# Spins into any idle bank, a first layer opened block by block, and later sums of weights, in a fused attention and feed-forward kernel

## The chip, the cores and the metric

The kernel runs on one core of one Trainium2 chip. The metric is the device time of one execution in microseconds. A core has five engines with queues of their own, which run in order and meet at semaphores: TensorE (PE in the profile; PEld is its loading of weights), VectorE (DVE), ScalarE (ACT), GpSimd (POOL) and SyncE (SP, which here issues the transfers). TensorE writes to eight banks of PSUM, b0 to b7, each of 512 columns of fp32; VectorE and ScalarE read them.

## The reference

```python
def _attn_ref(q, k, v, omega):          # batch 8, heads 8, 576 positions, head_dim 64, 128 features
    scale = 1.0 / np.sqrt(np.sqrt(D))
    q_s, k_s = (q * scale, k * scale)
    def phi(x):
        proj = np.einsum('bhsd,md->bhsm', x, omega)
        sq = np.sum(x * x, axis=-1, keepdims=True) / 2.0
        h = proj - sq
        h = h - np.max(h, axis=-1, keepdims=True)
        return np.exp(h) / np.sqrt(m)
    q_p, k_p = (phi(q_s), phi(k_s))
    kv = np.einsum('bhsm,bhsd->bhmd', k_p, v)
    z = np.sum(k_p, axis=2)
    num = np.einsum('bhsm,bhmd->bhsd', q_p, kv)
    den = np.einsum('bhsm,bhm->bhs', q_p, z)[..., None] + 1e-06
    return (num / den)
...
    xn = (x - mu) / np.sqrt(var + 1e-06) * g_ln      # x: 4608 rows of 512, the heads side by side
    ch = np.maximum(xn @ w_ch1, 0.0) @ w_ch2         # 512 -> 2048 -> 512
    return (x + ch)
```

## The kernel before, in words

The 4608 rows of x are worked in nine tiles of 512, each in four chunks of 128. For a tile, attention makes its part of x (keys: projection, maximum, exponent, products with the values into `kv`; queries: projection, a copy out of PSUM, a maximum over all partitions by GpSimd's all-reduce, a subtraction, an exponent, then the products with `kv` and a division). Then x is centred, turned (by TensorE in the first tile, line 1397) and split into a high and a low part, and the two layers follow. A matrix product in fp32 is made of three products of such parts. The weights come packed and are unpacked by VectorE and ScalarE, block by block: a block of w1 is 128 rows, `w1_00` to `w1_30` are the four that the first matmuls need. From the third tile on a scheme with seven products in place of eight is used (`seven`, line 1510), and for it sums of the w1 weights are made once (`gen_sides`, lines 496, 507 and 529) and kept in memory.

The order of every engine's work is made when the program is built, by a small scheduler (`Plan`). Each piece of work is a Python generator that yields what it needs: a result (`wait`), a buffer (`get`), or an engine with an estimated cost (`run`). Among what can start first on an engine, the lowest rank goes first. `plan.places` holds the free buffers, with the time since when each is free; `plan.cur.end` is the scheduled end of the work at hand. On the chip the engines then run that order and wait at semaphores, so the scheduler's costs set the order, not the time.

Until the first layer starts (`mlp_on`), TensorE's idle time is filled with spins: matmuls of a constant tile (`spin`, line 370) whose output nobody reads. `gen_warm` issues them one by one while nothing else could start, with a cost of 0.29 in the first 5 us and 0.11 later, and a single one follows most groups of products. They write `pw`, a tile in the last bank, which no other work may use until then.

The first layer of the first tile begins in `opening` (line 1448): four blocks of 128 hidden columns (`f`), each in its own bank, for the first two chunks of x (`j` = 0) and then for the last two. It waits for all four blocks of w1 before its first matmul. Later blocks of the first layer come from `mm1` (by `rounded`, line 1421, with 512 columns at once, or split into two matmuls of 256 columns at line 1480).

Of the kernel before, what the change touches and what calls it, by code (L numbers as in the profile page):

```python
# [12 lines left out]
F32 = mybir.dt.float32  # L13
# [6 lines left out]
PE, ACT, DVE, POOL, SP = "PE", "ACT", "DVE", "POOL", "SP"  # L20
PSUM = bass.MemoryType.PSUM

P = 128
# [5 lines left out]
NK = DM // P  # L29
# [6 lines left out]
T = 512  # L36
# [3 lines left out]
QB = 256  # L40
# [28 lines left out]
class Plan:  # L69
# [78 lines left out]
    def free(self, *names):  # L148
        for n in names:
            assert n not in self.places, n  # L150
            self.places[n] = self.cur.seen()
            self.cur.holds -= n[0] == "b" and 0 < self.cur.holds
            self.wake(lambda w: w[0] == "get" and n in w[1])
# [59 lines left out]
def favor_ffn(ctx, tc, kT, kTr, kD, kDr, vF, vR, qT, qD, omT, gT, w1, w2, out):  # L213
# [12 lines left out]
    nc = tc.nc  # L226
# [4 lines left out]
    ps = ctx.enter_context(tc.tile_pool(name="ps", bufs=1, space=PSUM))  # L231
    dp = ctx.enter_context(tc.tile_pool(name="dp", bufs=1, space=bass.MemoryType.DRAM))
    plan = Plan()
    free, done = plan.free, plan.done
# [16 lines left out]
    def us(eng, t):  # L251
        return "run", {eng: t}
# [16 lines left out]
    def wait(*key):  # L269
        return "wait", key  # L270

    def names(tag, n):
        return plan.own(*(f"{tag}{i}" for i in range(n)))

    def tile_of(tag, shape, dtype=F32, pool=None):
        pool = pool or (wp if tag[1].isdigit() and tag[0] == "w" else small if tag[0:2] in ("kv", "mb", "st") or tag[0] == "v" else sb)
        return pool.tile(shape, dtype, tag=tag, name=tag, bufs=1)
# [20 lines left out]
    banks = names("b", 8)  # L298
    plan.own("one", "two")
    b_at, b_h, b_acc = banks[0:2], banks[2:4], banks[4:8]  # L300
    mlp_on = []
# [27 lines left out]
    spin = const.tile([P, 2 * P], BF16, name="spin")  # L329
# [32 lines left out]
    nc.scalar.dma_start(g_sb, gT)  # L362
    nc.scalar.preload_act_table_set("natural_log_exp_and_others")

    pw = tile_of(banks[-1], [P, 512], F32, ps)[:, 0 : 2 * P]

    def warm(n):
        if not mlp_on:
            for _ in range(n):
                nc.tensor.matmul(pw, spin[:, 0:P], spin, start=True, stop=True)  # L370

    def gen_const():
        yield dma(P * M)
# [24 lines left out]
    wparts = {}  # L398
# [85 lines left out]
    def gen_sides(g, k):  # L484


        yield wait("xnT", SEVEN - 1, TC - 1)
        if g + k:
            yield wait("read", *((g, 0) if k else (g - 1, 1)))
        tags, parts = [], []  # L490
        for row in (k, k + 2):
            tags.append((yield "get", n_big))
            parts.append(tile_of(tags[-1], [P, 2, HC], F32R))
            yield dve2(DM)
            w = wparts[1, NK * g + row]
            nc.vector.tensor_tensor(out=f32(parts[-1]), in0=f32(w[:, :, 0]), in1=f32(w[:, :, 1]), op=ALU.add)
        for _ in range(2):
            tags.append((yield "get", n_big))
            parts.append(tile_of(tags[-1], [P, 2, HC], F32R))
        low, high, a, b = parts  # L500
        low, high, a, b = f32(low), f32(high), f32(a), f32(b)
        for out, left, right, op in (
            (a[:, 0], low[:, 1], high[:, 1], ALU.add), (a[:, 1], low[:, 0], low[:, 1], ALU.subtract),
            (b[:, 0], a[:, 0], low[:, 0], ALU.subtract), (b[:, 1], high[:, 0], b[:, 0], ALU.subtract),
        ):
            yield dve2(HC)
            nc.vector.tensor_tensor(out=out, in0=left, in1=right, op=op)
        if (g, 0) not in sides:
            sides[g, 0] = dp.tile([P, 4, 2, 2, 2, P], F32, tag=f"side{g}", name=f"side{g}", bufs=1)
        done(("read", g, k))  # L510
        for n in range(2):
            plan.add(plan.cur.rank, halved(g, k, n, tags[n], tags[2 + n], (a, b)[n]))
# [198 lines left out]
    def gen_k(b, c, kraw, v, early, t_v, n_kp):  # L711
# [52 lines left out]
        def side(s, t_b, pk):  # L764
# [3 lines left out]
            )  # L768
            if (b, c) in WIDE:
                o = kp[:, 4 * s : 4 * s + 4]  # L770
# [241 lines left out]
    def features(blk, j, s, t_b, pq):  # L1012
        t_c = yield "get", n_big
        qc = tile_of(t_c, [P, 2 * QB])
        eng = yield "run", {ACT: 0.48, DVE: 0.62} if blk >= T // QB else {ACT: 0.58}
        copy(eng, qc, pq)
        direct = blk < T // QB
        if not direct:
            free(t_b)
        mx_turn = yield "get", turn["mx"]  # L1020
        t_m = yield "get", n_big
        mx = tile_of(t_m, [P, 2 * QB])
        yield us(POOL, 1.8)
        nc.gpsimd.partition_all_reduce(mx, qc, P, bass_isa.ReduceOp.max)  # L1024
        done(("mx", blk, j, s))
        yield dve(2 * QB) if direct else dve2(2 * QB)
        nc.vector.tensor_tensor(out=qc, in0=pq if direct else qc, in1=mx, op=ALU.subtract)  # L1027
        if direct:
            free(t_b)
        free(t_m, mx_turn)  # L1030
        yield act(2 * QB, 1, 0.13)
        nc.scalar.activation(out=qc, in_=qc, func=AF.Exp)  # L1032
        phis[blk, j, s] = t_c, qc.rearrange("p (a b) -> p a b", b=QB)
        done(("phi", blk, j, s))
# [374 lines left out]
    def passes(x):  # L1409
        return x.rearrange("p (a c b) -> p c a b", b=BW, c=4)  # L1410
# [15 lines left out]
    def opening(count):  # L1426


        for k in range(NK):
            yield wait("w", 1, k)  # L1430
        ph = []
        for j in range(2):
            for i in range(2):
                yield wait("xnT", 0, 2 * j + i)
            if not mlp_on:
                mlp_on.append(True)
            xnT = xnTs[0][1]
            for f in range(count):
                if j == 0:
                    t_b = yield "get", b_h if f >= count - len(b_h) else b_acc  # L1440
                    ph.append((t_b, bank(t_b)))
                out = passes(ph[f][1])[:, :, 8 * j : 8 * j + 8]
                cs = slice(f % 2 * P, (f % 2 + 1) * P)
                for k in range(NK):
                    yield us(PE, 3 * 0.1134)
                    w = wparts[1, k][:, f // 2]
                    for l, r in ((0, 0), (1, 0), (0, 1)):
                        nc.tensor.matmul(  # L1448
                            out, w[:, l, cs],
                            passes(xnT[:, r, k])[:, :, 8 * j : 8 * j + 8],  # L1450
                            start=j + k + l + r == 0, stop=j == 1 and k == NK - 1 and r == 1, skip_group_check=True,
                        )
                if j == 1:
                    done(("mm1", 0, f))
                    plan.add(MOST_URGENT, relu(0, f, *ph[f]))
        in_order[0] = IN_ORDER
        paired(LONG)

    def mm1(t, f):
        for k in range(NK):  # L1460
            yield wait("w", 1, f // NK * NK + k)
        for i in range(TC):
            yield wait("xnT", t, i)
        if not mlp_on:
            mlp_on.append(True)
        t_x, xnT = xnTs[t]
        t_b = yield "get", b_h
        ph = bank(t_b)
        for k in range(NK):
            yield us(PE, 3 * 0.225)  # L1470
            w = wparts[1, f // NK * NK + k][:, f % NK // 2]
            cs = slice(f % 2 * P, (f % 2 + 1) * P)
            for l, r in ((0, 0), (1, 0), (0, 1)):
                first, last = k + l + r == 0, k == NK - 1 and r == 1
                if (t, f) < NARROWED and (fast[0] or locked[0] < 1) or as_rows(2 * ENOUGH):
                    rounded(ph, w[:, l, cs], xnT[:, r, k], start=first, stop=last, mixed=t == NARROWED[0], lies="a c b")
                    continue
                paired(2)
                for n in range(2):
                    nc.tensor.matmul(  # L1480
                        passes(ph)[:, :, 8 * n : 8 * n + 8], w[:, l, cs],
                        passes(xnT[:, r, k])[:, :, 8 * n : 8 * n + 8],
                        start=first and n == 0, stop=last, skip_group_check=True,
                    )
        if f == NF - 1:
            free(t_x)
        done(("mm1", t, f))
        plan.add(MOST_URGENT, relu(t, f, t_b, ph))
# [425 lines left out]
            free(t_x)  # L1914

    def gen_warm():
        plan.places.pop(banks[-1])
        plan.cur.after = 1.0
        while not mlp_on:
            cold = plan.cur.end < COLD  # L1920
            yield us(PE, 0.29 if cold else 0.11)
            warm(1)
            plan.cur.after = plan.cur.end + (0.0 if cold else WARM)
        free(banks[-1])

    def gen_mlp():
        last = []
# [54 lines left out]
        plan.add(min(rank, FRONT.get((n, f), rank)), gen_w(n, f, rank))  # L1982
    for g in range(NK):
        for k in range(2):
            plan.add(RSIDE + g, gen_sides(g, k))
        plan.add(URGENT, gen_move(g))
    for f in SHARED:
        plan.add(URGENT, gen_return(f))
# [40 lines left out]
LEAVE, RSIDE = 24, 24  # L2029
# [29 lines left out]
RX = -1100  # L2059
AHEAD = 0  # L2060
XACT = 3
WIDE = ((0, 0), (0, 2))
HELD = {0: (None, ("mx", 0, 0, 0)), 1: (("mx", 0, 1, 0), ("mx", 0, 1, 1)), 2: (None, None), 3: (None, None)}
RFIRST, BEHIND = (-35, -27.5), -33

# [50 lines left out]
```

## Time and profile before

| | |
|---|---|
| median of 3 runs | 909.66 us (909.53 to 909.95) |
| the profiled execution | 909.5 us, span 907.7 us |
| TensorE busy | 902.0 us (99%) |
| VectorE busy | 777.1 us (86%) |
| ScalarE busy | 543.2 us (60%) |
| GpSimd busy | 138.2 us (15%) |

The span is the time from the first to the last instruction of the profiled execution. Matmuls are pipelined and their ends are modelled in the profile, so a busy TensorE is one that has a matmul under way, not one at its peak. The granted clock of TensorE is 1.0 of full speed over the whole span.

### The profile page before, as it was taken

To read this page: it belongs to the slowest core of one execution; us is meant where nothing else is said; L and a number is where in the kernel's file an instruction comes from. 1 tells how busy PE (TensorE), PEld (TensorE's weight loads), DVE (VectorE), ACT (ScalarE), POOL (GpSimd) and SP (SyncE) were. 2 spreads that over 40 slices of the span, in tenths; PEclk is the share of its full clock that TensorE was granted. 3 is DMA by queue.
4 is the path that set the end of the run, shared out by engine and by line. 5 is a ranking of instruction groups with operands and counts; after the bars stand their busy time and mean duration, and the time that the engine had idled before them with its cause. 6 is when DMAs were issued, how large, how long until landed. Compare 5 with 4: busy or idle time off the path is not lost.

```text
span 907.7 us, 21830 instructions
## 1 busy us (share of the span) xinstructions
PE 902.0 (99%) x8159; PEld 822.2 (91%) x8159; DVE 777.1 (86%) x1799; ACT 543.2 (60%) x1303; POOL 138.2 (15%) x107
## 2 busy tenths in 40 slices
PE   9999999999999999999999999999999999999998
PEld 7888788888899999998999999999999999999998
DVE  6999988989888899779898998888878788778767
ACT  7988876546566477546774666556555553453442
POOL 4201503300112042000220131002301400000000
PEclk9999999999999999999999999999999999999999
DMA  9199665558898898988999988889777869998981
GB/s 349 70 352 363 242 201 173 150 146 261 291 349 287 281 366 270 307 296 288 299 338 310 329 278 273 307 296 357 233 230 237 292 180 325 374 318 295 360 293 48
DMA packets 153146, 249.92 MB, mean 275 GB/s; under 512 B 13264, under 2 KB 66640, under 8 KB 153040
## 3 DMA queue, kind: packets, MB, share of 16 engines
q1 hardware_dynamic: 152752, 248.45, 81.2%
q8 instruction: 65, 1.06, 0.5%
q14 instruction: 41, 0.34, 0.1%
q10 hardware_dynamic: 288, 0.07, 0.0%
HBM read 205.47 MB, written 42.99 MB: 274 GB/s over the span
## 4 chain that ended last, share of the span: by engine, by line
PE 96%; DVE 2%; DMA 1%; ACT 0%; issue 0%; ACTq 0%; DVEq 0%
PE b L1421 38%; PE b L1510 29%; PE b L1794 7%; PE b L1759 6%; PE b L827 4%; PE b L1187 4%; PE b L865 2%; PE b L909 2%; PE b L1448 1%; PE b L370 1%; PE b L957 1%; PE b L1099 1%; DVE v L1847 0%; DVE kp L1903 0%; DMA hid<-omT 0%; DMA w<-side 0%
## 5 line engine op out<-in xcount | busy, mean ns | idle before, releaser
L1421 PE MATMUL b<-w,hid 128*128 128x512 f32 x1090 | 261.9, 385 | 0.0
L1421 PEld LDWEIGHTS b<-w,hid 128*128 128x128 f32 x1090 | 198.9, 188 | 34.0 <-issue 0.3
L1024 POOL PARTITION_ALL_REDUCE wide<-wide x72 | 134.8, 1893 | 473.8 <-ACT wide L259 271.4
L1510 PE MATMUL b<-xnT,w 128*128 128x256 f32 x1344 | 174.0, 276 | 0.0
L1510 PEld LDWEIGHTS b<-xnT,w 128*128 128x128 f32 x1344 | 164.3, 188 | 2.8
L1510 PE MATMUL b<-w,w 128*128 128x256 f32 x1008 | 126.1, 276 | 0.0
L1574 DVE TENSOR_TENSOR w<-b,w 128x256 f32<-128x256 f32 x224 | 108.7, 485 | 15.9 <-PE b L1510 10.4
L1510 PEld LDWEIGHTS b<-w,w 128*128 128x128 f32 x1008 | 120.5, 188 | 1.5 <-DVE w L1574 0.3
L880 ACT ACTIVATE kp<-kp,mb 128x128 f32<-128x128 f32 x184 | 66.9, 397 | 34.0 <-DVE mb L877 33.7
L1421 PE MATMUL b<-xnT,w 128*128 128x512 f32 x324 | 79.4, 387 | 0.0
L1421 PEld LDWEIGHTS b<-xnT,w 128*128 128x128 f32 x324 | 59.7, 187 | 12.0 <-issue 1.0
L1032 ACT ACTIVATE wide<-wide 128x512 f32<-128x512 f32 x72 | 45.4, 635 | 37.7 <-DVE wide L1027 37.7
L1759 PE MATMUL b<-w,hid 128*128 128x256 f32 x460 | 64.4, 279 | 0.0
L1759 PEld LDWEIGHTS b<-w,hid 128*128 128x128 f32 x460 | 57.6, 188 | 1.4
L1600 ACT ACTIVATE hid<-w 128x256 fp32r<-128x256 f32 x85 | 40.4, 513 | 30.4 <-DVE w L1574 24.7
L259 ACT COPY wide<-b 128x512 f32<-128x512 f32 x69 | 39.4, 586 | 28.5 <-PE b L1421 20.0
L1794 PE MATMUL b<-w,wide 128*128 128x256 f32 x408 | 52.4, 275 | 0.0
L1602 DVE SCALAR_TENSOR_TENSOR hid<-w,hid 128x256 fp32r<-128x256 f32 x85 | 48.3, 586 | 4.1 <-ACT hid L1600 3.3
L1027 DVE TENSOR_TENSOR wide<-wide,wide 128x512 f32<-128x512 f32 x64 | 47.0, 743 | 3.6 <-POOL wide L1024 3.4
L986 DVE TENSOR_TENSOR wide<-wide,wide 64x512 fp32r<-64x512 f32 x56 | 40.8, 734 | 9.7 <-ACT wide L984 8.2
L1794 PEld LDWEIGHTS b<-w,wide 128*128 128x128 f32 x408 | 49.1, 188 | 0.0
L886 ACT COPY kp<-b 128x256 f32<-128x256 f32 x92 | 31.4, 368 | 24.0 <-PE b L865 23.8
(171 smaller groups left out, 1453.6 us busy)
## 6 DMA issues: line engine op xcount, KB each, us to landing
w<-side SPq DMA_DIRECT2D x224, 256.0 KB, 5.0
w<-kept SPq DMA_DIRECT2D x80, 512.0 KB, 5.2
w<-kept SPq DMA_DIRECT2D x67, 256.0 KB, 5.2
w<-w SPq DMA_DIRECT2D x32, 512.0 KB, 7.2
wide<-qD SPq DMA_DIRECT2D x56, 256.0 KB, 5.3
w<-deep SPq DMA_DIRECT2D x47, 256.0 KB, 5.5
wide<-kD SPq DMA_DIRECT2D x40, 256.0 KB, 5.1
kept<-w SPq DMA_DIRECT2D x16, 512.0 KB, 3.9
```

The lines of the kernel that those rows point to most:

```text
L880: nc.scalar.activation(out=kp[:, j], in_=kp[:, j], func=AF.Exp, scale=1.0, bias=mb[:, j : j + 1])
L986: nc.vector.tensor_tensor(out=qs[D:P], in0=qraw[D:P], in1=f32(qs[D:P]), op=ALU.subtract)
L1024: nc.gpsimd.partition_all_reduce(mx, qc, P, bass_isa.ReduceOp.max)
L1027: nc.vector.tensor_tensor(out=qc, in0=pq if direct else qc, in1=mx, op=ALU.subtract)
L1032: nc.scalar.activation(out=qc, in_=qc, func=AF.Exp)
L1421: nc.tensor.matmul(out.rearrange(f"p ({lies}) -> {order}", a=AW, b=BW), lhsT, rhs.rearrange(f"p (a c b) -> {order}", a=AW, b=BW), start=st ...
L1510: nc.tensor.matmul(passes(out), left(k, l), passes(right[:, r, k]), start=start and k + l + r == 0, stop=k + r == 2, skip_group_check=True,)
L1574: nc.vector.tensor_tensor(out=out, in0=left, in1=right, op=ALU.add)
L1600: nc.scalar.activation(out=hl[:, 0, cols], in_=x, func=AF.Relu)
L1602: nc.vector.scalar_tensor_tensor(out=hl[:, 1, cols], in0=x, scalar=0.0, in1=f32(hl[:, 0, cols]), op0=ALU.max, op1=ALU.subtract)
L1759: nc.tensor.matmul(accs[i].rearrange("p (c a b) -> p c a b", a=AW, b=BW)[:, :, n * 8 : n * 8 + 8], hl[:, l, cs], w[:, r, n * HC : (n + 1) ...
L1794: nc.tensor.matmul(out.rearrange("p (c a b) -> p c a b", a=8, b=8), left[:, l, chunk * P : (chunk + 1) * P], right[:, r].rearrange("p (a c ...
```

## The change

Spins get a new tile in the bank that has been free longest, by the scheduler's times, and are left out where no bank is free; the last bank is no longer set aside. A query copy of the first tile may also go to VectorE. `opening` waits for each block of w1 before the matmuls of that block and goes block by block in its first half; `mm1` waits likewise. The ranks of the sums of w1 weights are 12 apart instead of 1. In the first batch, key chunk 3 instead of chunk 2 gets the exponent in one wide piece (`WIDE`).

```diff
-    pw = tile_of(banks[-1], [P, 512], F32, ps)[:, 0 : 2 * P]
-
-    def warm(n):
-        if not mlp_on:
+    def warm(n, at=0.0):
+        idle = [] if mlp_on else [x for x in banks if plan.places.get(x, 1e9) <= plan.cur.end - at]
+        if n and idle:
+            to = bank(min(idle, key=plan.places.get), 2 * P)
             for _ in range(n):
-                nc.tensor.matmul(pw, spin[:, 0:P], spin, start=True, stop=True)
+                nc.tensor.matmul(to, spin[:, 0:P], spin, start=True, stop=True)
...
-        eng = yield "run", {ACT: 0.48, DVE: 0.62} if blk >= T // QB else {ACT: 0.58}
+        eng = yield "run", {ACT: 0.48, DVE: 0.62} if blk >= T // QB else {ACT: 0.58, DVE: 0.62}
...
     def opening(count):
-        for k in range(NK):
-            yield wait("w", 1, k)
...
-            for f in range(count):
+            places = [(k, f) for k in range(NK) for f in range(count)]
+            for k, f in places if j == 0 else sorted(places, key=lambda x: x[1]):
                 if j == 0:
+                    yield wait("w", 1, k)
+                if j == k == 0:
...
     def mm1(t, f):
-        for k in range(NK):
-            yield wait("w", 1, f // NK * NK + k)
...
         for k in range(NK):
+            yield wait("w", 1, f // NK * NK + k)
...
     def gen_warm():
-        plan.places.pop(banks[-1])
...
-            yield us(PE, 0.29 if cold else 0.11)
-            warm(1)
+            cost = 0.29 if cold else 0.11
+            yield us(PE, cost)
+            warm(1, cost)
             plan.cur.after = plan.cur.end + (0.0 if cold else WARM)
-        free(banks[-1])
...
-            plan.add(RSIDE + g, gen_sides(g, k))
+            plan.add(RSIDE + 12 * g, gen_sides(g, k))
...
-WIDE = ((0, 0), (0, 2))
+WIDE = ((0, 0), (0, 3))
```

On TensorE, at the very start, the first spins of the kernel before (`b7_93` is the one tile that all of them write; `DVE_49` is VectorE's semaphore):

```order
L370 LDWEIGHTS spin_74 [waits DVE_49]
L370 MATMUL b7_93<-spin_74 128x256
L370 LDWEIGHTS spin_74
L370 MATMUL b7_93<-spin_74 128x256
L370 LDWEIGHTS spin_74
L370 MATMUL b7_93<-spin_74 128x256
```

The same place in the change (`b0_114`, `b0_116` and so on are new tiles in one bank, b0; `PE_49` is TensorE's own semaphore):

```order
L370 LDWEIGHTS spin_74 [waits DVE_49]
L370 MATMUL b0_114<-spin_74 128x256
L370 LDWEIGHTS spin_74
L370 MATMUL b0_116<-spin_74 128x256 [waits PE_49]
L370 LDWEIGHTS spin_74
L370 MATMUL b0_119<-spin_74 128x256 [waits PE_49]
L370 LDWEIGHTS spin_74
L370 MATMUL b0_121<-spin_74 128x256 [waits PE_49]
```

There are 13 spins at this place in both; eleven of them now wait for a value of TensorE's semaphore that the spin just before sets (the first has none before it, and at the tenth the bank changes).

On TensorE, ahead of the fifth product of x (line 1099), the end of a burst of 17 spins in the kernel before:

```order
L370 LDWEIGHTS spin_74
L370 MATMUL b7_93<-spin_74 128x256
L370 LDWEIGHTS spin_74
L370 MATMUL b7_93<-spin_74 128x256
L1099 MATMUL b0_594<-kv0_94,wide2_335 64x65 [waits Activation_49]
```

And in the change, the end of a burst of 18 at the same place:

```order
L370 LDWEIGHTS spin_74
L370 MATMUL b0_570<-spin_74 128x256 [waits PE_49]
L370 LDWEIGHTS spin_74
L370 MATMUL b3_575<-spin_74 128x256 [waits DVE_49]
L370 LDWEIGHTS spin_74
L370 MATMUL b3_577<-spin_74 128x256 [waits PE_49]
L370 LDWEIGHTS spin_74
L370 MATMUL b3_580<-spin_74 128x256 [waits PE_49]
...
L1099 MATMUL b0_594<-kv0_93,wide2_352 64x65 [waits Activation_49]
```

The bursts are about as long as before here, and 16 of the 18 spins wait for the one before. In the whole program there are 64 spins instead of 101: 13, 5, 18, 8 and 9 in bursts and 11 single ones.

On TensorE, where the first layer opens, before:

```order
L1397 MATMUL b5_712<-ident_76,wide10_693 128x128 x3
L1448 MATMUL b6_710<-xnT0_624,w1_00_369 128x4x8x8 [waits DVE_49,PE_49]
L1448 MATMUL b6_710<-xnT0_624,w1_00_369 128x4x8x8
L1448 MATMUL b6_710<-xnT0_624,w1_00_369 128x4x8x8 [waits DVE_49]
L1448 MATMUL b6_710<-xnT0_624,w1_10_493 128x4x8x8 x3
L1448 MATMUL b6_710<-xnT0_624,w1_20_539 128x4x8x8 x3
L1448 MATMUL b6_710<-xnT0_624,w1_30_625 128x4x8x8 x3
```

And in the change:

```order
L370 MATMUL b6_721<-spin_74 128x256 [waits PE_49]
L1448 MATMUL b6_724<-xnT0_627,w1_00_452 128x4x8x8 [waits PE_49,Activation_49]
L1448 MATMUL b6_724<-xnT0_627,w1_00_452 128x4x8x8
L1448 MATMUL b6_724<-xnT0_627,w1_00_452 128x4x8x8 [waits DVE_49]
L1448 MATMUL b4_734<-xnT0_627,w1_00_452 128x4x8x8 x3
L1448 MATMUL b2_739<-xnT0_627,w1_00_452 128x4x8x8 x3
L1448 MATMUL b3_743<-xnT0_627,w1_00_452 128x4x8x8 x3
L1448 MATMUL b6_724<-xnT0_627,w1_10_517 128x4x8x8 x3
```

One block of w1 now serves four banks before the next block is touched, a burst of 9 spins stands just ahead, and the transposes of the third chunk (line 1397), ahead of the opening before, come after its first 24 matmuls.

## Rows read from the trace of the kernel before

**Rows 1.** The page: busy time, share of the span; granted clock in 40 slices.
```profile
PE 902.0 (99%) x8159; PEld 822.2 (91%) x8159; DVE 777.1 (86%) x1799; ACT 543.2 (60%) x1303; POOL 138.2 (15%) x107
...
PEclk9999999999999999999999999999999999999999
```

**Rows 2.** All waits of TensorE: us in total, times, longest.
```profile
PE b L370 <- DVE spin L330: 1.2, 1, 1.2
PE b L1397 <- ACT wide L1262: 0.2, 1, 0.2
```

**Rows 3.** The chain of waits in order of time: start us, us, what.
```profile
42.07 8.52 PE b L1448 x75
...
210.37 25.11 PE b L1421 x114
...
558.79 2.73 PE b L1510 x24
```

**Rows 4.** Timeline of TensorE from the start: start us, us, instructions.
```profile
1.19 2.95 PE L370 MATMUL b<-spin 128*128 128x256 bf16 x13 [1.19 <-DVE spin L330]
4.22 1.85 PE L909 MATMUL b<-om,w 64*128 64x128 f32 x16
5.91 1.03 PE L957 MATMUL b<-wide,om 64*128 64x256 f32 x8
6.78 2.49 PE L909 MATMUL b<-om,w 64*128 64x128 f32 x32
```

**Rows 5.** Timeline of TensorE, 24 to 52 us.
```profile
25.53 1.48 PE L370 MATMUL b<-spin 128*128 128x256 bf16 x12
26.95 0.69 PE L1099 MATMUL b<-kv,wide 128*64 128x65 f32 x16
...
30.06 2.03 PE L370 MATMUL b<-spin 128*128 128x256 bf16 x17
32.02 0.69 PE L1099 MATMUL b<-kv,wide 128*64 128x65 f32 x16
...
34.30 0.28 PE L370 MATMUL b<-spin 128*128 128x256 bf16 x1
34.42 0.60 PE L1397 MATMUL b<-ident,wide 128*128 128x128 f32 x4
...
35.57 1.27 PE L370 MATMUL b<-spin 128*128 128x256 bf16 x10
36.67 0.60 PE L1397 MATMUL b<-ident,wide 128*128 128x128 f32 x4
37.11 1.25 PE L370 MATMUL b<-spin 128*128 128x256 bf16 x10
...
38.98 2.64 PE L1448 MATMUL b<-xnT,w 128*128 128x256 f32 x21
```

**Rows 6.** Timeline of all engines, first 40 us: VectorE's and ScalarE's first readers.
```profile
6.11 1.29 DVE L766 TENSOR_REDUCE mb<-b 128x4 f32<-128x512 f32 x2 [1.94 <-PE b L909]
...
6.97 1.07 ACT L259 COPY wide<-b 128x512 f32<-128x512 f32 x2 [4.03 <-PE b L957]
```

**Rows 7.** Timeline of ScalarE, 24 to 42 us.
```profile
37.31 0.58 ACT L1400 CAST xnT<-b 128x512 fp32r<-128x512 f32 x1 [0.23 <-PE b L1397]
```

**Rows 8.** Timeline of GpSimd: the second, third and fourth pair of all-reduces.
```profile
12.48 3.77 POOL L1024 PARTITION_ALL_REDUCE wide<-wide  x2 [1.28 <-ACT wide L259]
19.35 3.58 POOL L1024 PARTITION_ALL_REDUCE wide<-wide  x2 [3.10 <-ACT wide L259]
25.16 3.75 POOL L1024 PARTITION_ALL_REDUCE wide<-wide  x2 [2.23 <-DVE w L420]
```

**Rows 9.** Timeline of all engines, 32 to 62 us: the last step of w1's fourth block.
```profile
34.16 0.72 DVE L446 SCALAR_TENSOR_TENSOR w<-wide,g_sb,w 128x512 fp32r<-128x512 f32 x1
```

**Rows 10.** Groups by line, VectorE, 150 to 245 us: busy us, mean ns.
```profile
L496 DVE TENSOR_TENSOR wide<-w 128x512 f32<-128x512 f32 x16 | 13.0, 811 | 0.1
```

More of the change, by code (lines that the diff above doesn't have):

```diff
@@ L1443, in opening @@
                 cs = slice(f % 2 * P, (f % 2 + 1) * P)
-                for k in range(NK):
[L1445 to L1453, printed above, removed]
+                yield us(PE, 3 * 0.1134)
+                w = wparts[1, k][:, f // 2]
+                for l, r in ((0, 0), (1, 0), (0, 1)):
+                    nc.tensor.matmul(
+                        out, w[:, l, cs],
+                        passes(xnT[:, r, k])[:, :, 8 * j : 8 * j + 8],
+                        start=j + k + l + r == 0, stop=j == 1 and k == NK - 1 and r == 1, skip_group_check=True,
+                    )
+                if j == 1 and k == NK - 1:
                     done(("mm1", 0, f))
@@ L1459, in mm1 @@
     def mm1(t, f):
-        for k in range(NK):
-            yield wait("w", 1, f // NK * NK + k)
         for i in range(TC):
```

## The prediction, made before the result was known

> **What bounds the kernel now.** I read the page first: TensorE is busy for 99% of the span at the full granted clock [rows 1]. A busy TensorE need not be one that never waits, so the list of its waits came next: in 907.7 us it waits 1.4 us by that list, and both entries lie before 39 us [rows 2]. The chain of waits agrees: from the opening of the feed-forward part on it consists of matmul groups that follow each other, at 220 ns for a matmul of 512 columns (25.11/114) and 114 ns for one of 256 (2.73/24) [rows 3]. So the kernel has two parts. Up to 38.98 us, where the first matmul of line 1448 starts [rows 5], the attention of the first tile is made, and spins (line 370) fill TensorE. After it some 865 us of matmuls run without a hole, and a tail of a few us ends it. What the change does to the start of line 1448 goes into the total one to one; in the long part it could only cost, by a stall.
>
> **What the change does to a spin.** Now all spins write one tile, which nobody frees, and they stream: 13 in 2.95 us at the start, where they are twice as long as later, so about 0.21 us apart [rows 4]; 12 in 1.48 us later, 0.11 us apart, while a single one lasts 0.28 us from start to end [rows 5]. In the change every spin asks for a new tile in the bank that has been idle longest. The scheduler doesn't count the spin as a use of that bank, so the next spin takes the same bank again, and the order of the built program shows what follows: the second matmul waits for TensorE's own semaphore, that is for the end of the spin just before it. Of 64 spins 45 wait so, and four real matmuls behind a spin do as well: two key projections, the first product of x and the first matmul of line 1448.
>
> No row of before shows TensorE waiting for its own last matmul. From below the wait costs nothing (0.11 us apart as now). From above it costs what any reader of a bank pays: ScalarE starts 0.03 us after the end of the projection that ended at 6.94 (5.91 + 1.03) [rows 4, 6], and 0.04 us after the transposes that ended at 37.27 [rows 5, 7]. A waiting spin would then come 0.28 + 0.03 = 0.31 us after the one before. A semaphore is raised by the same matmul end for TensorE as for a reader, so I take 0.31, and 0.11 for a spin that doesn't wait. At the start, with 0.21 us of streaming, 0.21 + (0.31 - 0.11) = 0.41 us.
>
> **The sum, by TensorE's order in the change.**
> Start: 13 spins, 11 of which wait: 11 x 0.41 + 2 x 0.21 = 4.9 us, from 1.19 to 6.1 instead of 4.1. The projection of the first keys now starts at 4.22 [rows 4]; it starts 2.0 us later, and VectorE's first reduction, which waits for it, at 8.1 instead of 6.11 [rows 6].
>
> From there to the end of the key products (now 25.53, where the burst of 12 spins begins [rows 5]), 19.4 us now. Three edits work here: bank b7 is free for real work, two query copies move from ScalarE to VectorE (0.61 us each, the spacing of the reductions [rows 6]), and another key chunk gets the wide exponent. I walked the new orders of VectorE, ScalarE, GpSimd and TensorE against each other with the durations of the rows. Stations: VectorE has finished the first key chunk at 10.4; GpSimd's first four all-reduces of 1.8 us end at 17.0; VectorE's fourth subtraction ends at 18.5 and frees the bank into which the next spin writes, so TensorE stands there for 0.6 us; the last query projections run to 20.9, and four key products and two of the remainder follow at 0.62 us each, less than one waits for, to 24.5. That is 16.4 us, 3.0 less than now; what is saved are GpSimd's waits of 3.10 and 2.23 us ahead of its third and fourth pair [rows 8] and a burst of 12 spins. Bounds: no gain (27.5) and twice the gain (21.5); I take the walk, 24.5.
>
> From there TensorE's own order decides:
> 5 spins and the first product, five waits: 5 x 0.31 = 1.6, to 26.1.
> Four products of x with three spins between: 3.1 (as now from 26.95 to 30.06, the first four of eight), to 29.2.
> 18 spins, 16 wait: 5.2, to 34.4. Now 17 spins take 1.96 (30.06 to 32.02).
> Three products, the first transposes and the last product: now 32.02 to 35.57, 3.6, to 38.0.
> 8 spins, 6 wait: 2.1, to 40.1. Second transposes 0.44 (36.67 to 37.11), to 40.5.
> 9 spins and the first matmul of line 1448, nine waits: 2.8, to 43.3.
> (All durations of now from [rows 5].)
> The data are there earlier: the second chunk's centring, the last input of the second transposes, ends at about 38.7 by the same walk, so spins and not data set 43.3. Against 38.98 the opening starts 4.3 us later.
>
> **The other edits.** Opening block by block of the weights: the fourth block of w1 is ready now at 34.88 [rows 9], four us before the opening, so the earlier wait bought nothing to give back; the 96 matmuls are the same, and if a block came late in the new order, it has 1.4 us (12 x 0.114) of matmuls per block as cover. Worth 0. The same goes for the wait per block in the later first-layer groups. The sums of the w1 weights (lines 496 to 529) move by rank; on VectorE they still stand ahead of the seven-product tiles that read them, and end about as early in its order as now. Their 16 first sums cost 13.0 us of VectorE [rows 10], hidden below TensorE; were one late, the first groups of line 1510 would wait, a few us at most. A TensorE that is 4 us late gives VectorE more room, so 0. Last, the scheduler splits more first- and second-layer matmuls: 43 of 512 columns fewer, 86 of 256 more, everything else equal in number: 43 x (2 x 114 - 220) = 0.3 us.
>
> Sum: the profiled execution's 909.5 + 4.3 + 0.3 = 914.1; its time lies 0.16 below the median shown, so 914.2.
>
> **Rivals.**
> The spins are the gain (other side). If a spin that follows its like costs 0.11 us as now, nothing is lost at the start, the walk ends at 22.5, and the bursts shrink to 0.55, 2.0, 0.9 and 1.0: TensorE could open at 34.1, but the second chunk's x, its centring and its split into two parts follow one another on VectorE and ScalarE and hold it until about 36. That is 3.0 earlier, 909.5 - 3.0 + 0.3 = 906.9. With 11 waits at the start and 36 behind the walk the opening stands at 34.1 + 47 x (spacing - 0.11), so it decides at a spacing of 0.21 us, where that reaches 38.98. For it speaks that the wait for the own engine might end at issue; against it that every reader in the rows starts after the end.
>
> The clock drops. Within a burst TensorE would stream 0.11 of every 0.31 us, and only 0.21 of 0.41 at the start, while now it streams without holes there and the clock is full in all slices [rows 1]. [...] No row of before has such sparse work, so nothing excludes it.
> [...]
>
> No difference: the waits cost 0.31, but the walk to 24.5 is 4 us too long (the projections being ahead of what I gave VectorE), and the two cancel. 909.5 +- 1.8.
>
> **How the numbers follow.** 0.2% is 1.8 us, about what a measurement of this kernel can tell from none. Forecast 0.58 (its own range 911.5 to 917.5: the walk's two bounds move it by 3 us each way), clock 0.17, spins free 0.15, no difference 0.10. So faster 0.15, same 0.10, slower 0.75. The time is the forecast's, 914.2. The range must reach to both sides: 907 takes in half of the case of free spins, 919.5 a third of the clock's; about 0.19 stays outside.
>
> **What the profile after would show.** Line 370: 64 spins, 0.31 us apart in bursts; at the start about 0.41 apart and the first line 909 near 6.2. The burst of 18 near 29 to 34. First matmul of line 1448 at 43.3, with the end of the span moved by the same amount. TensorE's list of waits between 45 and 900 us still empty. I would be wrong if line 1448 starts before 39 us (spins 0.11 apart, or readers that were never ready sooner), if the clock row shows digits below 9 in the first two slices, or if TensorE waits in the long part, at lines 1510 or 1421, where the sums of weights come late.

## The result, and the profile after

The changed kernel takes 921.8 us (median of 6 executions, 918.77 to 924.15) against 909.99 us: 1.28% more, ratio 1.0128, 95% interval 1.0104 to 1.0153. It is slower, as forecast; the forecast of 914.2 us and its range, up to 919.5, were too low. The profiled execution is the shortest of the six, 918.77 us with a span of 917.0 us and a mean granted clock of 1.000. The means of the six are 1.000, 0.993, 0.997, 0.996, 0.994 and 1.000, in the order of 918.77, 923.43, 920.17, 923.65, 924.15 and 919.38 us. So there are two losses to explain: 9.3 us that stand in the profiled execution, and some 1 to 5 us more in the executions whose clock fell. In the experiments below one of the eleven executions with spins that reuse their tile took 2964.36 us, and its ratio leaves it out.

The page of the profiled execution, busy time and granted clock, which answers to [rows 1]:

```profile
PE 906.4 (99%) x8165; PEld 821.0 (90%) x8165; DVE 777.0 (85%) x1801; ACT 543.8 (59%) x1315; POOL 139.1 (15%) x107
...
PEclk9999999999999999999999999999999999999999
```

Its timeline of TensorE up to the first matmuls of line 1421 (start us, us, instructions), which answers to [rows 4, 5]:

```profile
1.19 5.30 PE L370 MATMUL b<-spin 128*128 128x256 bf16 x13 [1.19 <-DVE spin L330]
6.42 2.08 PE L909 MATMUL b<-om,w 64*128 64x128 f32 x16
8.29 1.88 PE L957 MATMUL b<-wide,om 64*128 64x256 f32 x8
...
11.79 1.03 PE L957 MATMUL b<-wide,om 64*128 64x256 f32 x8
...
19.17 1.16 PE L909 MATMUL b<-om,wide 64*128 64x128 f32 x14 [0.94 <-DVE w L727]
...
25.23 1.16 PE L827 MATMUL b<-v,w 64*64 64x65 f32 x64
26.61 1.57 PE L370 MATMUL b<-spin 128*128 128x256 bf16 x5 [0.22 <-DVE wide L1027]
28.33 0.69 PE L1099 MATMUL b<-kv,wide 128*64 128x65 f32 x16
...
31.44 5.59 PE L370 MATMUL b<-spin 128*128 128x256 bf16 x18
36.97 0.69 PE L1099 MATMUL b<-kv,wide 128*64 128x65 f32 x16
...
40.52 2.34 PE L370 MATMUL b<-spin 128*128 128x256 bf16 x8
42.70 0.60 PE L1397 MATMUL b<-ident,wide 128*128 128x128 f32 x4
43.13 2.87 PE L370 MATMUL b<-spin 128*128 128x256 bf16 x9
46.16 2.96 PE L1448 MATMUL b<-xnT,w 128*128 128x256 f32 x24
48.96 0.60 PE L1397 MATMUL b<-ident,wide 128*128 128x128 f32 x4
...
58.03 5.47 PE L1421 MATMUL b<-w,hid 128*128 128x512 f32 x24
```

The 13 spins of the start now take 5.30 us instead of 2.95, and the first line 909 stands at 6.42 instead of 4.22. The later spins stand 0.326 us apart: the 18 from 31.44 to 36.97 take 5.53 us, where 17 took 1.96 [rows 5]. The page calls TensorE 99% busy all the same, since a spin of 0.27 us fills most of the 0.326 us that one of them costs: the loss can't be seen in the busy time. The opening (line 1448) starts at 46.16 instead of 38.98, 7.2 us later. Line 1421 follows at 58.03 instead of 50.43, 7.6 later, since the third chunk's transposes (48.96) now lie inside the opening and stood ahead of it before. The last matmul ends 9.3 us later.

The clock has a part in this execution too, at the very start. The trace's record of the granted clock begins at 10.01 us here, and at 5.70 us in the kernel before; in both kernels the 1.000 and the row of nines count what lies ahead of the record as full. Ahead of it TensorE runs at half pace: the eight matmuls of line 957 take 1.88 us at 8.29 (two start every 0.427 us) and 1.03 us at 11.79 (every 0.216 us), and 1.03 us at 5.91 in the kernel before [rows 4]. So lines 909 and 957 take 3.57 us from 6.42 to 9.99, against 2.56 us before (4.22 to 6.78): of the 3.2 us that are lost by then, 1.0 is a clock that rose later.

All waits of TensorE (us in total, times, longest), which answers to [rows 2]:

```profile
PE b L370 <- DVE spin L330: 1.2, 1, 1.2
PE b L909 <- DVE w L727: 0.9, 1, 0.9
PE b L827 <- ACT kp L784: 0.6, 1, 0.6
PE b L1421 <- DVE kp L888: 0.6, 2, 0.4
PE b L370 <- DVE wide L1027: 0.2, 1, 0.2
```

The waits of the spins for each other are not in it. By the profile's modelled ends, a spin of 0.27 us leaves TensorE idle for 0.05 us until the next one starts, and no wait in these lists is shorter than 0.15 us. Only the spacing of the spins shows them.

### The profile page after: what moved, and what is told of

It reads as the page before. It is cut to its first block, busy times and chain, and to the rows that moved or that the text cites. A ratio compares the mean times of both kernels' runs of the same rounds, so it can differ in the third digit from the quotient of the medians.

```text
span 917.0 us, 21861 instructions
## 1 busy us (share of the span) xinstructions
PE 906.4 (99%) x8165; PEld 821.0 (90%) x8165; DVE 777.0 (85%) x1801; ACT 543.8 (59%) x1315; POOL 139.1 (15%) x107
## 4 chain that ended last, share of the span: by engine, by line
PE 92%; DVE 5%; ACT 1%; DMA 1%; issue 1%; POOL 0%; ACTq 0%; DVEq 0%
PE b L1421 35%; PE b L1509 28%; PE b L1793 7%; PE b L1758 6%; PE b L1187 4%; PE b L827 3%; PE b L865 2%; PE b L370 2%; PE b L1448 1%; PE b L909 1%; PE b L1479 1%; PE b L957 1%; DMA w<-kept 1%; PE b L1099 1%; DVE w L1573 0%
## 5 line engine op out<-in xcount | busy, mean ns | idle before, releaser
L1421 PE MATMUL b<-w,hid 128*128 128x512 f32 x1065 | 254.3, 384 | 0.0
L1509 PEld LDWEIGHTS b<-xnT,w 128*128 128x128 f32 x1344 | 165.1, 188 | 3.3
L1421 PE MATMUL b<-xnT,w 128*128 128x512 f32 x306 | 76.5, 389 | 0.0
L1758 PE MATMUL b<-w,hid 128*128 128x256 f32 x510 | 69.6, 278 | 0.0
L1421 PEld LDWEIGHTS b<-xnT,w 128*128 128x128 f32 x306 | 56.0, 187 | 11.4 <-issue 1.0
L1027 DVE TENSOR_TENSOR wide<-wide,wide 128x512 f32<-128x512 f32 x64 | 49.6, 779 | 2.7 <-POOL wide L1024 2.5
L1254 ACT ACTIVATE wide<-x,mvs 128x512 f32<-128x512 f32 x28 | 35.1, 1264 | 15.2 <-DVE mvs L1150 7.0
L986 DVE TENSOR_TENSOR wide<-wide,wide 64x512 fp32r<-64x512 f32 x56 | 38.5, 700 | 6.1 <-ACT wide L984 4.8
```

Source lines behind the costliest of these rows:

```text
L1421: nc.tensor.matmul(out.rearrange(f"p ({lies}) -> {order}", a=AW, b=BW), lhsT, rhs.rearrange(f"p (a c b) -> {order}", a=AW, b=BW), start=st ...
L1509: nc.tensor.matmul(passes(out), left(k, l), passes(right[:, r, k]), start=start and k + l + r == 0, stop=k + r == 2, skip_group_check=True,)
L1758: nc.tensor.matmul(accs[i].rearrange("p (c a b) -> p c a b", a=AW, b=BW)[:, :, n * 8 : n * 8 + 8], hl[:, l, cs], w[:, r, n * HC : (n + 1) ...
```

## The experiments

The table has the ratio to the kernel before, timed on the same chip in the same job, and from each profiled execution the start of the opening and the time from the start of the first matmul of line 1421 to that of the last matmul.

| kernel | us | ratio, 95% interval | opening at | behind 1421 |
|---|---|---|---|---|
| before | 909.99 | | 38.98 | 853.0 |
| the change | 921.8 | 1.0128 (1.0104 to 1.0153) | 46.16 | 854.6 |
| spins reuse their tile | 910.67 | 1.0007 (0.9998 to 1.0016) | 36.02 | 856.0 |
| spin edit alone | 931.4 | 1.0232 (1.0218 to 1.0246) | 54.12 | 858.1 |
| all but the spin edit | 913.83 | 1.0037 (1.0024 to 1.0050) | 40.34 | 856.7 |
| spins in two banks | 911.62 | 1.0016 (1.0007 to 1.0025) | 37.13 | 856.3 |
| reuse, sums 1 apart | 912.76 | 1.0040 (1.0028 to 1.0053) | 36.61 | 858.5 |
| reuse, old opening | 918.69 | 1.0102 (1.0086 to 1.0117) | 38.66 | 863.0 |
| reuse, both of these | 916.75 | 1.0084 (1.0070 to 1.0098) | 38.33 | 860.1 |
| before + reusing spins | 913.34 | 1.0046 (1.0033 to 1.0059) | 37.51 | 857.8 |
| reuse, half the spins | 910.8 | 1.0017 (1.0008 to 1.0026) | 35.97 | 856.1 |
| reuse, old wide chunk | 913.2 | 1.0046 (1.0033 to 1.0060) | 35.82 | 857.3 |
| reuse, old copies | 914.71 | 1.0061 (1.0048 to 1.0073) | 36.91 | 857.8 |
| the change again | 921.77 | 1.0131 (1.0115 to 1.0148) | 48.73 | 855.1 |

**Spins that reuse their tile.** A spin takes a new tile only where other work has had the bank since; the order of all instructions stays that of the change.

```diff
     def tile_of(tag, shape, dtype=F32, pool=None):
+        spun.pop(tag, None)
...
-            to = bank(min(idle, key=plan.places.get), 2 * P)
+            tag = min(idle, key=plan.places.get)
+            to = spun[tag] if tag in spun else bank(tag, 2 * P)
+            spun[tag] = to
```

> The change, with one thing taken back: a spin that follows a spin in the same bank writes the same tile again, so none of the 64 spins waits for TensorE's own semaphore (52 did). Order, banks and number of spins stay. Theory 1 (the waits between spins are the loss): spins 0.11 us apart in bursts, 0.21 at the start, first line 909 near 4.2, first matmul of the opening at 36.5 to 39 instead of 46.16, time 909 to 912 us, granted clock 1.0 in every execution. Theory 2 (the other edits, the new order of copies, weights and sums, cost as much): the time stays above 914 us with the spins dense. Theory 3 (the missing spins let the clock fall, not the waits): times still spread over several us with a mean clock below 1.0.

Measured: 910.67 us, mean clock 0.999 or 1.000 in every execution. Its timeline of TensorE (its lines stand 5 lower: 375 is 370, 1453 is 1448):

```profile
1.19 2.95 PE L375 MATMUL b<-spin 128*128 128x256 bf16 x13 [1.19 <-DVE spin L333]
4.15 1.16 PE L914 MATMUL b<-om,w 64*128 64x128 f32 x16
...
21.51 1.17 PE L832 MATMUL b<-v,w 64*64 64x65 f32 x64
22.90 0.71 PE L375 MATMUL b<-spin 128*128 128x256 bf16 x5 [0.22 <-DVE wide L1032]
...
26.86 1.49 PE L375 MATMUL b<-spin 128*128 128x256 bf16 x12
28.85 0.81 PE L375 MATMUL b<-spin 128*128 128x256 bf16 x6 [0.50 <-DVE wide L1032]
29.59 0.69 PE L1104 MATMUL b<-kv,wide 128*64 128x65 f32 x16
...
36.02 3.05 PE L1453 MATMUL b<-xnT,w 128*128 128x256 f32 x24
...
48.16 5.81 PE L1426 MATMUL b<-w,hid 128*128 128x512 f32 x24
```

With the same spins in the same places and only their waits gone, the opening comes 10.1 us earlier than in the change, and 3.0 us earlier than before. Theory 1 holds: the waits are the loss, with what the clock makes of them. Of the 10.1 us, 2.3 stand at the first line 909 (4.15 against 6.42) and 3.7 at the burst of five (22.90 against 26.61): most of the 1.4 between is the half pace, since the record of the clock begins at 4.05 us here. Yet the time is that of the kernel before within its interval: what is won ahead of the opening is given back behind it, which the next runs look at.

**The spin edit alone**, on the kernel before (new `warm` and `gen_warm`, nothing else).

```diff
-    pw = tile_of(banks[-1], [P, 512], F32, ps)[:, 0 : 2 * P]
...
+            to = bank(min(idle, key=plan.places.get), 2 * P)
             for _ in range(n):
-                nc.tensor.matmul(pw, spin[:, 0:P], spin, start=True, stop=True)
+                nc.tensor.matmul(to, spin[:, 0:P], spin, start=True, stop=True)
```

> The kernel before with the spin edit alone: 76 spins, 66 of them with a wait for TensorE's own semaphore, in bursts of 13, 6, 20, 23 and 4. Theory 1: spacing 0.31 us in bursts and 0.41 at the start, line 909 near 6.4, the opening 6 to 10 us later than 38.98, time 915 to 922 us, and a mean clock below 1.0 in some executions. Theory 2 (the other edits cost): 909 to 912 us.

Measured: 931.4 us, above the range of theory 1, with a mean clock of 0.991 to 0.993 in every execution. Two rows of its timeline of TensorE:

```profile
31.17 6.45 PE L370 MATMUL b<-spin 128*128 128x256 bf16 x20
37.55 1.14 PE L1099 MATMUL b<-kv,wide 128*64 128x65 f32 x16
```

Its windows (us, their length, the busy times of the engines, and behind POOL's the granted clock):

```profile
26.00:31.00 5.00, 4.57 (x77) 2.90 (x73) 4.77 (x13) 5.00 (x14) 4.17 (x4) 1.00 0.04 12
...
37.50:43.50 6.00, 6.00 (x72) 4.81 (x71) 2.87 (x11) 2.47 (x7) 0.00 (x0) 0.50 0.01 3
...
51.90:58.00 6.10, 5.93 (x30) 5.06 (x30) 3.76 (x7) 3.50 (x6) 0.00 (x0) 0.57 0.00 0
58.00:70.00 12.00, 12.00 (x95) 11.54 (x95) 10.69 (x18) 11.00 (x20) 0.00 (x0) 1.00 0.71 239
```

The granted clock falls from 1.00 to 0.50 near the end of the burst of 20 spins, and again in that of 23 (44.51 to 51.92), ahead of the opening; 16 products then take 1.14 us instead of 0.69.

**The kernel before with reusing spins** is the same order once more, with the waits taken out as above.

```diff
-            to = bank(min(idle, key=plan.places.get), 2 * P)
+            tag = min(idle, key=plan.places.get)
+            to = spun[tag] if tag in spun else bank(tag, 2 * P)
+            spun[tag] = to
```

> The kernel before with nothing changed but that spins go to any idle bank and reuse their tile there: 76 spins, no waits between them, the same order as the spin edit alone (931.4 us). Theory 1 (the waits are the whole loss of the spin edit, the clock's fall included): 907 to 911 us, clock 0.999 or 1.0 in every execution. If the idle bank itself cost something (fewer spins where no bank is idle, first spins that wait for a reader), 912 us or more.

Measured: 913.34 us, clock 1.0 in four executions and 0.997 in one, opening at 37.51. So of the 2.3% of the spin edit alone, 1.9 are the waits and the clock that falls with them. The 913.34 us lie above the 907 to 911 us of theory 1, where the other theory put a cost of the idle bank; but the opening is 1.5 us earlier than before, and the loss stands behind it, in the 857.8 us of the table.

**All but the spin edit**: the change with the spins, `warm` and `gen_warm` of before.

```diff
-            to = bank(min(idle, key=plan.places.get), 2 * P)
...
+    pw = tile_of(banks[-1], [P, 512], F32, ps)[:, 0 : 2 * P]
...
+                nc.tensor.matmul(pw, spin[:, 0:P], spin, start=True, stop=True)
```

> The change with the spins of before (one tile in the last bank, set aside): all other edits stay. 109 spins, none waits. Theory 1: 909 to 912 us, clock 1.0 in every execution, with up to 1.5 us lost by the third chunk's transposes that now lie inside the opening and by more 256-column matmuls. Theory 2 (the other edits cost): above 914 us.

Measured: 913.83 us, between the two theories. The other edits are not free in this schedule: the opening comes at 40.34, 1.4 later, and the part from line 1421 on takes 3.7 us more.

**Spins in two banks**, turn by turn, each with a new tile, so that a spin waits for the one before the last.

```diff
+            idle.sort(key=plan.places.get)
-            to = bank(min(idle, key=plan.places.get), 2 * P)
+            to = bank(idle[len(spins) % min(2, len(idle))], 2 * P)
+            spins.append(1)
```

> The change with spins that alternate between the two banks that have been idle longest, so that a spin waits for the end of the one before the last. If the wait is for the end of a matmul 0.28 us long plus 0.03, two spins fit into 0.31 us: spacing 0.155 to 0.17 in bursts, the 18-burst 2.9 us instead of 5.5, the opening about 5 us earlier than 46.16, time 911 to 915 us. If a wait for the own semaphore costs a fixed time whatever it waits for, spacing stays 0.31 us and the time 918 to 924 us.

Measured: 911.62 us, clock 0.999 or 1.000. From its timeline of TensorE:

```profile
27.73 2.89 PE L374 MATMUL b<-spin 128*128 128x256 bf16 x18
...
37.13 2.96 PE L1452 MATMUL b<-xnT,w 128*128 128x256 f32 x24
```

18 spins up to 30.54 take 2.81 us; their starts stand 0.109 and 0.217 us apart by turns, 0.326 us for two. So the price is not that of a wait as such: it is the time to the end of the matmul that is waited for, 0.326 us from its start. Two banks halve it, and the clock holds. The opening comes 9.0 us earlier than in the change, not about 5, since nothing is lost at the start either: there two spins fit into 0.43 us, no slower than at half pace without waits, and the record of the clock begins at 4.20 us.

**Half the spins**: the first experiment with another cost of a spin in the scheduler; all other instructions stay in the same order.

```diff
-            cost = 0.29 if cold else 0.11
+            cost = 0.29 if cold else 0.22
```

> The change with spins that reuse their tile, and only about half of them in the bursts (3, 9, 4 and 5 in place of 5, 18, 8 and 9); every other instruction in the same order. Theory 1 (with dense spins the data set the opening, the spins are cover): the opening within 0.3 us of 36.02, holes in TensorE's list of waits where the spins were, 910 to 911.5 us; if the granted clock falls in the holes, 913 us or more. Theory 2 (the spins still set it): the opening at 33.9 to 35, time 908.5 to 909.8 us.

Measured: 910.8 us, clock 0.999 or 1.000. From its timeline of TensorE:

```profile
29.24 0.38 PE L375 MATMUL b<-spin 128*128 128x256 bf16 x2 [1.24 <-DVE wide L1032]
29.55 0.69 PE L1104 MATMUL b<-kv,wide 128*64 128x65 f32 x16
...
35.97 0.48 PE L1453 MATMUL b<-xnT,w 128*128 128x256 f32 x2
36.67 2.78 PE L1453 MATMUL b<-xnT,w 128*128 128x256 f32 x22 [0.22 <-DVE xnT L1407]
```

Where nine spins are gone TensorE waits 0.7 us longer, and the next product starts at 29.55 instead of 29.59. The subtraction that it waits for ended 0.4 us later in this execution (29.24 against 28.85), so the shorter burst is worth up to that much, not the 1 to 2 us of theory 2. With dense spins it is mostly the data that set the opening, at about 36 us, and the spins are cover; in the change the spins are late themselves.

**The other edits, each taken back on the reusing spins.** Four runs undo one each, in this order: the ranks of the sums, the opening with `mm1`, the wide chunk, and the copies on VectorE. A fifth undoes the first two together.

```diff
-            plan.add(RSIDE + 12 * g, gen_sides(g, k))
+            plan.add(RSIDE + g, gen_sides(g, k))
```

```diff
+        for k in range(NK):
+            yield wait("w", 1, k)
...
-            places = [(k, f) for k in range(NK) for f in range(count)]
-            for k, f in places if j == 0 else sorted(places, key=lambda x: x[1]):
+            for f in range(count):
...
+        for k in range(NK):
+            yield wait("w", 1, f // NK * NK + k)
```

```diff
-WIDE = ((0, 0), (0, 3))
+WIDE = ((0, 0), (0, 2))
```

```diff
-        eng = yield "run", {ACT: 0.48, DVE: 0.62} if blk >= T // QB else {ACT: 0.58, DVE: 0.62}
+        eng = yield "run", {ACT: 0.48, DVE: 0.62} if blk >= T // QB else {ACT: 0.58}
```

> The change with spins that reuse their tile (as in the first experiment, 910.67 us), and the ranks of the sums of w1 weights 1 apart again. In the first experiment the opening began at 36.02, 2.96 us before that of the kernel before, yet the end was no earlier: the part behind the opening lost 3.7 us. Theory 1 (the later sums cost it, by a later VectorE order): opening unchanged at 36.0, time 907 to 908.5 us. Theory 2 (the part behind the opening loses by its start, transposes inside the opening and a slower rhythm of matmuls, whatever the sums do): 910 to 911.5 us.

> The change with spins that reuse their tile, and the opening and the later first-layer groups as before (wait for all blocks of w1 first, hidden block by hidden block). The built order has 23 spins ahead of the opening instead of 9, so if the opening by weight blocks buys an earlier start, the first matmul of the opening comes 1.0 to 1.6 us later than 36.02 and the time is 911 to 912.3 us. If it buys nothing, as the prediction had it, the start is within 0.3 us of 36.0 and the time 910 to 911 us, or lower by up to 0.4 us because the third chunk's transposes stand ahead of the opening again.

> The change with spins that reuse their tile, and key chunk 2 instead of 3 with the wide exponent, as before. The prediction gave this edit no price of its own; the built order has 20 instead of 18 spins in the third burst and 12 instead of 9 in the last, so the opening should come 0.3 to 1.0 us later than 36.02. If it matters no more than that: 910.5 to 912.5 us. If the wide exponent on chunk 3 is what brings the opening forward: an opening after 38 us and 913 us or more.

> The change with spins that reuse their tile, and all query copies of the first tile on ScalarE, as before. The built order has 34 spins instead of 18 in the third burst and one instead of 8 in the next, so ScalarE is the late engine there: the opening 1 to 2.5 us later than 36.02, time 911.5 to 914 us. If the copies on VectorE buy nothing: opening within 0.3 us of 36.02 and 910 to 911.5 us.

> Both of the two edits before at once (sums 1 apart, opening and later groups as before), on spins that reuse their tile; left of the change are the spins, the copies that may go to VectorE and the wide exponent. Theory 1 (late sums cost 2 to 3 us): 908 to 909.5 us. Theory 2 (they cost nothing): within 0.5 us of the kernel with the old opening alone.

Measured, in this order: 912.76, 918.69, 913.2, 914.71 and 916.75 us. Each is slower than the 910.67 us with all edits, and none beats the kernel before. The first four lie above the ranges expected (the 913.2 us of the wide chunk fit only the theory of an opening after 38 us, and it came at 35.82); the fifth fits neither theory, 1.9 us below the old opening alone. From the list of TensorE's waits with the sums 1 apart (line 1514 is 1510 of the kernel before):

```profile
PE b L1514 <- DVE hid L1606: 1.0, 2, 0.6
...
PE b L1514 <- DVE w L1391: 0.4, 2, 0.2
PE b L1514 <- ACT w L259: 0.4, 1, 0.4
...
PE b L1514 <- DVE xnT L1391: 0.3, 1, 0.3
...
PE b L1104 <- PE b L375: 0.2, 1, 0.2
```

From the same list with the old opening (line 1515 is 1510):

```profile
PE b L1515 <- ACT w L259: 4.2, 1, 4.2
```

The last row of the first list is a wait of TensorE for its own spin, long enough to be listed. With the sums 1 apart, TensorE waits 2.1 us at line 1514, where the kernel with the ranks of the change waits nothing: the later sums are a gain there, not the cost that was suspected. With the old opening it is the other way: there the sums 1 apart are 1.9 us faster (916.75 against 918.69), and the wait for ScalarE is 0.7 us instead of 4.2. With the old opening alone TensorE starts the opening 2.6 us later: 14 more spins stand ahead of it (1.5 us), and 1.1 us stand already at the burst of five (24.01 against 22.90), up to which the order is the same and only the clock's record begins later, at 7.15 us. In the same way all of the 0.6 us with the sums 1 apart stand there already (23.51). With the old opening TensorE stands 4.2 us up to 455 us, for data that ScalarE makes late; near the end of that hole the granted clock falls to 0.50, up to 461 us. With the old wide chunk and the old copies the opening starts 0.2 us earlier and 0.9 us later, and halts inside for 0.8 and 0.6 us, for a chunk of x that VectorE splits late. How much of each loss belongs to the edit and how much to the new order that the scheduler makes around it, these runs can't tell.

**The change again**, unaltered, for its clock.

> The changed kernel once more, unaltered, for its clock. Its profiled execution took 918.8 us with the granted clock at 1.0 throughout, while four of its six executions had a mean of 0.993 to 0.997 and 920.2 to 924.2 us. Theory 1 (the clock falls behind the sparse bursts, as in the kernel with the spin edit alone): each execution with a mean below 0.998 takes 920 us or more and each at 1.0 takes 918 to 920; where the profiled one has the lower mean, its trace shows a granted clock of 0.5 behind the burst of 18 spins or the two after it, with products of 1.1 us for 16 in place of 0.69. Theory 2 (the clock falls elsewhere, in the part behind the opening): the first 58 us stay at 1.0 and the fall stands later.

Measured: 921.77 us, mean clock 0.996 to 0.998 in all four executions. From the profiled one, 921.89 us, windows (columns as above):

```profile
33.00:34.00 1.00, 0.83 (x4) 0.30 (x4) 1.00 (x2) 1.00 (x5) 0.00 (x0) 1.00 0.00 0
...
35.00:36.00 1.00, 0.89 (x4) 0.32 (x4) 0.41 (x1) 1.00 (x3) 0.00 (x0) 0.50 0.00 0
...
40.00:41.00 1.00, 1.00 (x15) 0.65 (x13) 0.78 (x4) 0.66 (x1) 0.00 (x0) 0.50 0.00 0
41.00:42.00 1.00, 1.00 (x18) 0.88 (x17) 0.07 (x1) 0.00 (x0) 0.00 (x0) 0.58 0.07 16
42.00:43.00 1.00, 1.00 (x21) 0.83 (x19) 0.75 (x3) 0.43 (x1) 0.00 (x0) 1.00 0.00 0
```

Its timeline of TensorE:

```profile
31.64 6.38 PE L370 MATMUL b<-spin 128*128 128x256 bf16 x18
37.96 1.14 PE L1099 MATMUL b<-kv,wide 128*64 128x65 f32 x16
...
42.46 0.69 PE L1099 MATMUL b<-kv,wide 128*64 128x65 f32 x16
...
48.73 2.97 PE L1448 MATMUL b<-xnT,w 128*128 128x256 f32 x24
```

Theory 1: the clock falls inside the burst of 18, while TensorE does nothing but waiting spins, and is back near 42 us. The opening starts 2.6 us later than in the execution whose clock did not fall (48.73 against 46.16), 2.4 of it behind the start of this burst (31.64 against 31.44); the part behind line 1421 is as long, within 0.5 us.

## Why the prediction was right and wrong

**The mechanism was right.** A spin behind a spin in the same bank waits for its end: 0.326 us apart against 0.31 predicted, 0.427 at the start against 0.41, 0.11 where the wait is gone. The bursts of 18 and 9 took 5.5 and 3.0 us against 5.2 and 2.8, and the stretches between them were as predicted. The first and the fifth experiment settle it: without the waits the same program opens at 36.02 us, the "about 36" that the rival of free spins named, and with two banks the price is halved.

**The first step that failed is the chance of the clock, 0.17.** In ten executions of the change it fell in eight, 1 to 5 us on top of the 9 us; only the two others, 918.77 and 919.38 us, lie inside the range. No row bears out the 0.17: no row of before has TensorE at work that sparse, as the prediction said itself. Nor does a run bear out that the range takes in a third of this case: all eight lie above 919.5 us. What the fall costs stands in the trace of the change again: the granted clock is 0.50 from 35 to near 42 us, from inside the burst of 18 on, and 1.00 behind, and the opening comes 2.6 us later. At 0.50 it takes 1.07 us from the start of a product (line 1099) to the next start instead of 0.61, three quarters more. With the same order and spins that don't wait the mean clock was 0.999 or 1.000 in every execution, and so it was with spins that take two banks by turns.

**Where the clock did not fall the sum was still 4.7 us short**, 914.1 against 918.77, in four terms.
- The walk to the end of the key products: 16.4 us from the first reduction (8.1 to 24.5); measured 17.9 (8.53 to 26.39). It saves 1.5 us of the 19.4 before, not 3.0, and with the late first reduction that is 1.9. The walk moved the first projections by the 2.0 us of the spins and kept their pace of before; they start 2.2 us later and then take 3.57 us instead of 2.56, at half pace up to 10.0 us. A clock that rises later behind the waiting spins, with a record that begins at 10.01 us instead of 5.70, was in no term. So GpSimd's first four all-reduces end at 18.6 instead of 17.0, and TensorE stands 0.94 us up to 19.17 for VectorE, where the walk had 0.6.
- From there to the opening: 19.8 us instead of 18.8, over half of it the 0.326 in place of 0.31 in 34 waits of spins, 0.2 the 0.42 us ahead of the two matmuls that wait for a spin, and 0.2 a wait of the first spin for a reader of its bank.
- The third chunk's transposes: 0.4 us inside the opening. The order that the prediction was made from shows them move, and the sum left them out.
- Behind line 1421: 1.7 us where 0.3 was given for splits. By the starts of the matmuls, two intervals of 0.56 and 0.78 us in place of 0.22, the waits for VectorE (line 888), cost 0.9, the splits 0.5 and the seven-product matmuls of line 1509 0.4; line 865 gains 0.2. The list of waits there was to stay empty.

**The other edits at nothing** was wrong, though not visibly in this result. Opening block by block "bought nothing to give back" only because the spins of the change were late; with dense spins the old opening costs 0.95% (a ratio of 1.0102 against 1.0007), about half of it the one hole of 4.2 us. The same holds for the ranks of the sums (0.33%), the wide chunk (0.39%) and the copies (0.54%), each with what its new order brings. And on the spins of before all of them together lose 0.37%.

**Left open** is why the part behind line 1421 takes 854.6 to 863 us in all these kernels and 853 in the kernel before. In the kernel with reusing spins it is 3.0 us: 2.6 in matmuls of 512 columns and their splits, 0.4 in line 1510. No version here beats the kernel before.

## What to carry to other kernels

In this kernel a tile that is made anew for each write is a wait for the last write to its bank, also on the engine that made both (a spin every 0.326 us, against 0.16 in two banks by turns and 0.11 in one tile): filler that is meant to stream needs one tile, or at the least two banks in turn. A busy share of 99% doesn't show this; the spacing of the starts does. A start that comes earlier is worth nothing until the part behind it, in the order that it then has, has been shown not to give it back.

## What the runs showed of the hardware

The granted clock fell to 0.50 though TensorE was busy for 0.83 us of each us by the profile, in waiting spins 0.326 us apart; whether it fell differed between executions of one program (1.000 to 0.993), and with 0.16 us on average between spins it stayed at 0.999 or 1.000 in all of 11. A mean of 0.997 is also there in one of five executions of the kernel before with reusing spins, of which there is no trace.

The first rise of the clock differs as well. In the three traces whose first spins wait at 0.427 us, its record begins at 9.38, 10.01 and 11.11 us, in the eleven others between 3.98 and 7.15. What comes behind moves with it: in six kernels whose order is the same up to there and whose start loses nothing to waits, the record begins at 4.05, 4.20, 5.06, 5.49, 5.85 and 7.15 us, and the burst of five starts at 22.90, 22.89, 23.30, 23.51, 23.68 and 24.01 us. So a start of the opening, taken from one execution each, can't be told from another within about 1 us.

In these runs matmuls of 512 columns have two rhythms, which last for whole groups without any wait in the list: 220 ns and about 230 ns. The 24 of line 1421 that follow the opening took 5.47 us in the change (58.03, above) and 5.81 us with reusing spins (48.16, above), at a granted clock of 1.00 in both; in the latter 331 of the 1507 intervals that follow a matmul of that line lie between 225 and 245 ns, against 245 of 1507 in the change and 240 of 1550 before. What sets it was not found.
